# Which attention units keep whole fp32 operands, and what the plan counts for turning weights

## The chip, the cores and the metric

The kernel runs on one core of one Trainium2 chip. The metric is the device time of one execution in microseconds (us), as the median of several runs. A core has a matrix engine (PE, whose weight loads are listed apart as PEld), a vector engine (DVE), a scalar engine (ACT), GpSimd (POOL), a sync engine (SP) that issues the DMAs here, and 16 DMA engines.

## The reference, cut to what matters

```python
def _attn_ref(q, k, v, n_sink, window):          # batch 4, heads 8, sequence 768, head size 64
    scores = scale * np.matmul(q, k.transpose(0, 1, 3, 2))
    keep = is_sink | in_window                    # 4 sink columns, a causal window of 128
    scores = np.where(keep, scores, -1000000000.0)
    a = softmax(scores)
    return np.matmul(a, v)

def _moe_ref(x, w_gate, w_val, w_out):            # 3072 tokens, 512 wide, 1536 inside
    gate = 1.0 / (1.0 + np.exp(-(x @ w_gate)))
    val = x @ w_val
    return gate * val @ w_out
```

All arithmetic is to be good to fp32; the weights arrive as 64-bit floats, two 32-bit words each.

## The kernel before, in words

**Units and chunks.** Attention is cut into 96 units, numbered `u`: one head of one block of 256 queries. Eight units (the eight heads) fill one token block of 256 rows; there are 12 blocks. The feed-forward part takes the blocks in chunks (`CHUNKS`): four chunks of one block, then four of two. The chunks of two (`PAIRS`) use a scheme with sums and differences of blocks and weights, which needs further weight tiles (`thirds`) and sums of the blocks' inputs (`second_half`).

**Two ways to multiply.** An fp32 product can run on the matrix engine with whole fp32 operands, or with operands split into a high and a low part of the type fp32r, where two or three products are summed. The splitting (`copy` for the high part, `rest` for the low one) is work for ACT, DVE and POOL.

- A unit with `u < PLAIN` (line 45) is **plain**. Its queries and keys, its weights (the softmax output) and its values are whole fp32. `load` (line 875) brings 64 partitions of `qkT`; the scores of a tile are one fp32 product; `turn` (line 1043) transposes the two weight tiles and the sink columns on the matrix engine; `pv` (line 1127) multiplies, and two heads share one PSUM bank `xr`, from which the feed-forward input is taken.
- Any other unit is **split**. `load` brings 128 partitions of `qkT`, that is, twice the bytes. Then come `hi` and `kl` (lines 920 to 928), the scores as two fp32r products, `st`, `turned` and `sk` for the sinks (lines 1012 to 1035), `turn` with two transposes, a high and a low part of the weights (`wt`, lines 1071 to 1083), `vhl` (line 1093), `pv` in fp32r against the split sink values `VSHL` (line 858), and three small steps that add the parts (`low`, `xf`, lines 1155 to 1188).

**Start of the program.** While attention runs, 36 blocks of weights arrive (`wst`, three buffers) and are decoded from 64-bit floats by `decode` (line 1253): two steps on ACT (the second nearly always there), two on DVE. Chunk 0 (`feed_whole`, line 1394) multiplies with whole fp32 weights as they are decoded, and its groups of products stand ahead of those of chunk 1 in a fixed order (`GROUPS`). Its inputs `X0` sit meanwhile in one of the two buffers of `hi` and in one of `xf`. `halves` (line 1331) splits the decoded weights, and stores the low parts in DRAM (`wlo_d`), from where chunks 1 and later fetch them (`lo`).

**The order of work.** Nothing is issued in the order of the program text. A planner (`Plan`, line 313) simulates the engines with a duration that is written at each step, a priority and the buffers, and emits a fixed order for every engine. The priorities around the change: decoding 8 to 15.2, a unit its own number `u`, `halves` 16 to 25.9, the feed-forward steps of ACT, DVE and POOL below all of these numbers (first), and the matrix engine's feed-forward products last (10000 and up), so that they fill what attention leaves. The durations in the plan decide only the order; on the chip each engine runs its list and waits where it must.

**The sinks** (line 838) are stored in two tiles `VS0` for plain units, and in tiles `VSHL` for split ones, four heads each. Both kinds take the same two `vshl` buffers, so a `VSHL` tile can be filled only when the last plain unit is through.

Of the kernel before, what the change touches and what calls it, by code (L numbers as in the profile page):

```python
# [41 lines left out]
TSTEP = 8000.0  # L42
THIRDS = 130000.0
CROWDED = 350000.0
PLAIN = 20
SINKP = -2.0
SCALP = -0.5
SKSWAP = 0
# [501 lines left out]
def kernel(  # L550
# [36 lines left out]
    class Late:  # L587
# [5 lines left out]
        def tile(self, *args, **kw):  # L593
            if self.pool is None:
                first.close()
                self.pool = main.enter_context(tc.tile_pool(name="p3", bufs=1))
            return self.pool.tile(*args, **kw)
# [10 lines left out]
    plan = Plan()  # L608

    class InOrder:  # L610
# [9 lines left out]
    PE, V, A, G, Q = (  # L620
        InOrder(e) for e in (nc.tensor, nc.vector, nc.scalar, nc.gpsimd, nc.sync)
    )
# [19 lines left out]
    def dma(prio, ns, fn, r=(), w=(), start=0.0, behind=None):  # L642
        return plan.op(prio, [("Q", ISSUE, fn)], r, w, dma=ns, start=start, behind=behind)

    def copy(prio, cols, out, in_, r, w, psum=False, start=0.0, apart=False):

        plan.op(
            prio,
            [
                ("A", act(cols, psum), lambda: A.copy(out=out(), in_=in_())),  # L650
                ("V", vec(cols) if psum or apart else one(cols), lambda: V.tensor_copy(out=out(), in_=in_())),
            ],
            r, w, start=start,
        )

    def rest(prio, cols, out, in0, in1, r, w, psum=False):

        plan.op(
            prio,
            [  # L660
                (
                    "G", pool(cols), lambda: G.tensor_tensor(
                        out=out(), in0=in0(), in1=in1().bitcast(F32), op=ALU.subtract
                    ),
                ),
                (
                    "V", vec(cols) if psum else two(cols), lambda: V.tensor_tensor(
                        out=out(), in0=in0(), in1=in1().bitcast(F32), op=ALU.subtract
                    ),
                ),  # L670
            ][1 if psum else 0 :],
            r, w,
        )
# [146 lines left out]
    def zero(prio, tile, cols, ap, part=None):  # L820

        def fill():
            x = ident[128 - ap().shape[0] :, 0:1]
            while len(x.shape) < len(ap().shape):
                x = x.unsqueeze(1)
            A.mul(out=ap(), in_=x.broadcast_to(list(ap().shape)), mul=0.0)

        plan.op(
            prio, [("A", act(cols), fill)], w=[tile if part is None else (tile, part)],
        )  # L830
# [7 lines left out]
    def sinks(b, u):  # L838
        if not b:
            for y in range(2):  # L840
                for x in V0:
                    zero(u + 0.5 + y, x[y], 3 * D, lambda x=x, y=y: x[y]()[:, :, (1 - y) * D : (2 - y) * D], 4)
            for x in SK0:
                zero(u + 0.4, x, 128, x)
            for x in VS0:
                zero(u + 0.3, x, H * D, x)
            for t, x in enumerate(VS0):
                for y in range(2):
                    o = 64 * y + NS * t
                    dma(  # L850
                        u + 0.5, 91.0, lambda x=x, y=y, o=o: Q.dma_start(
                            out=x()[o : o + NS, :, y * D : y * D + D],
                            in_=v[b, y::2, 0:NS, :].rearrange("h p d -> p h d"),
                        ), w=[(x, o)],
                    )
        raw = tile([128, H, D], F32, "w2", BUFS["w2"])
        for i in range(0 if b else 1, 2):
            VSHL[b, i] = tile([128, H // 2, 2 * D], F32R, "vshl", 2, const)
        u = max(u, PLAIN) + SINKP
        for o in range(0, 128, NS):  # L860
            dma(
                u, 91.0, lambda o=o: Q.dma_start(
                    out=raw()[o : o + NS], in_=v[b, :, 0:NS, :].rearrange("h p d -> p h d"),
                ), [READY2], [(raw, o)] + [VSHL[b, i] for i in range(2) if b and (b, i) in VSHL],
            )
        for i in range(0 if b else 1, 2):
            hs = slice(i * H // 2, i * H // 2 + H // 2)
            both = VSHL[b, i]
            x, hi = lambda hs=hs: raw()[:, hs], lambda both=both: both()[:, :, 0:D]
            copy(u, H // 2 * D, hi, x, [raw], [both, READY2])  # L870
            rest(
                u, H // 2 * D, lambda both=both: both()[:, :, D : 2 * D], x, hi, [raw, both], [both]
            )
# [15 lines left out]
    def attend(u, b, h, t0, T, XR):  # L889
# [6 lines left out]
        if h == 0 and t0 == 0:  # L896
            sinks(b, u)
        plain = u < PLAIN
        y = h % 2
# [32 lines left out]
        P = tile([128, T, KW], F32, "P", BUFS["P"])  # L932
# [104 lines left out]
        tp = tile([128, 512], F32, "a", BUFS["a"], ps)  # L1037
        Z = 1 if plain else 2
        wt = tile([128, 2, T, 2, 128], F32 if plain else F32R, "wt", BUFS["w"])
# [27 lines left out]
                channel_multiplier=-1,  # L1067
            )

        plan.op(u, [("PE", 30 + (T + plain) * 110, turn)], [P], [tp, wt], busy=0.45)  # L1070
        plan.op(
            u, [("A", act(W, True), lambda: A.copy(out=w()[:, 0, :, 1], in_=tpv()))], [tp], [(wt, 0)]
        )
# [115 lines left out]
        if y:  # L1189
# [8 lines left out]
            elif not pair_of[tn]:  # L1198
# [3 lines left out]
                i = half if wide else c % 2  # L1202
# [466 lines left out]
    u = 0  # L1669
    ci = 0  # L1670
    for b in range(B):
        t0 = 0
        for T in AT[b]:
            XR = [None]
            for h in range(H):
                attend(u, b, h, t0, T, XR)
                u += 1
            t0 += T
            n = u // H - 1
            if pair_of[n]:  # L1680
                (second_half if n == CHUNKS[ci][1] else first_half)(n)
            if n == CHUNKS[ci][-1]:
                feed(ci)
                ci += 1
# [74 lines left out]
```

## Time and profile before

| | us |
|---|---|
| median of 3 runs | 773.53 |
| lowest and highest run | 773.02, 774.98 |
| span of the profiled execution | 774.4 |

The span runs from the first to the last instruction of the profiled execution. Engine times in the rows are busy times in that execution; a matrix instruction is pipelined, so its listed duration overlaps the next one's, and its real price is the distance from its start to the next start. Nearly all work shows line 618, where a helper records each operation, so the rows are told apart by tile names: `a` is a PSUM bank of attention, `m` and `o` are those of the feed-forward part, `wst` and `ws` are weights being decoded and held, `w<-o` is an output leaving PSUM.

### The profile page before, as it was taken

To read this page: it belongs to the slowest core of one execution; us is meant where nothing else is said; L and a number is where in the kernel's file an instruction comes from. 1 tells how busy PE (TensorE), PEld (TensorE's weight loads), DVE (VectorE), ACT (ScalarE), POOL (GpSimd) and SP (SyncE) were. 2 spreads that over 40 slices of the span, in tenths; PEclk is the share of its full clock that TensorE was granted. 3 is DMA by queue.
4 is the path that set the end of the run, shared out by engine and by line. 5 is a ranking of instruction groups with operands and counts; after the bars stand their busy time and mean duration, and the time that the engine had idled before them with its cause. 6 is when DMAs were issued, how large, how long until landed. Compare 5 with 4: busy or idle time off the path is not lost.

```text
span 774.4 us, 16292 instructions
## 1 busy us (share of the span) xinstructions
PE 748.7 (97%) x4986; PEld 677.2 (87%) x4986; DVE 608.8 (79%) x1781; ACT 473.2 (61%) x1338; POOL 504.3 (65%) x647
## 2 busy tenths in 40 slices
PE   7999999999899999999999999999999999999995
PEld 6877766899799899989999998999999999999994
DVE  5889988996789999968998999778999884433332
ACT  7889888665676777836656675557776652322221
POOL 3654665887899899946777987557976855311210
PEclk9999999999999999999999999999999999999999
DMA  6898987999899876776777786867697655776662
GB/s 164 225 299 255 327 255 223 358 302 307 295 316 315 281 225 217 213 255 211 239 247 232 218 257 213 255 193 245 201 302 250 192 165 180 219 238 216 192 212 79
DMA packets 120878, 185.57 MB, mean 240 GB/s; under 512 B 23248, under 2 KB 45264, under 8 KB 120784
## 3 DMA queue, kind: packets, MB, share of 16 engines
q1 hardware_dynamic: 120784, 184.45, 75.6%
q8 instruction: 42, 0.69, 0.4%
q14 instruction: 52, 0.43, 0.2%
HBM read 159.24 MB, written 25.17 MB: 238 GB/s over the span
## 4 chain that ended last, share of the span: by engine, by line
PE 59%; DVE 10%; DMA 9%; POOL 3%; ACT 2%; issue 1%; SPq 0%; POOLq 0%; ACTq 0%; DVEq 0%
PE m L618 32%; PE a L618 16%; PE o L618 10%; DMA lo<-wlo_d 3%; DMA out_dram<-w 2%; DVE ws L618 2%; DMA qkT<-in_qk_dram 2%; DVE P L618 1%; DMA vraw<-in_vt_dram 1%; POOL ws L618 1%; DVE th L618 1%; POOL wt L618 1%; DVE hi L618 1%; DMA wst<-in_moe_w_val_dram 1%; DVE xf L618 1%
## 5 line engine op out<-in xcount | busy, mean ns | idle before, releaser
L618 PE MATMUL m<-ws,ws 128*128 128x256 f32 x1536 | 290.2, 285 | 0.2 <-ACT th L618 0.2
L618 PE MATMUL m<-ws,lo 128*128 128x256 f32 x1344 | 288.8, 283 | 1.7 <-DMA lo<-wlo_d 1.6
L618 PEld LDWEIGHTS m<-ws,ws 128*128 128x128 f32 x1536 | 246.1, 190 | 11.9 <-issue 0.5
L618 PEld LDWEIGHTS m<-ws,lo 128*128 128x128 f32 x1344 | 215.6, 189 | 2.6 <-DMA lo<-wlo_d 2.5
L618 POOL TENSOR_SCALAR_AFFINE_SELECT wt<-wt 128x512 fp32r<-128x512 f32 (+3 forms) x192 | 124.9, 652 | 43.2 <-DVE wt L618 19.4
L618 POOL TENSOR_TENSOR gl<-th,gh 128x512 fp32r<-128x512 f32 (+1 forms) x34 | 38.1, 1121 | 102.2 <-ACT gh L618 83.5
L618 ACT ACTIVATE P<-P,negm_all 128x144 f32<-128x144 f32 x192 | 79.0, 412 | 30.4 <-DVE negm_all L618 29.3
L618 ACT ACTIVATE th<-m 128x256 f32<-128x256 f32 x96 | 36.7, 382 | 76.1 <-DVE th L618 71.3
L618 DVE TENSOR_TENSOR cv<-m,cv 128x256 f32<-128x256 f32 x96 | 40.1, 418 | 50.0 <-ACT cv L618 32.8
L618 ACT CAST gh<-th 128x512 fp32r<-128x512 f32 (+1 forms) x82 | 42.9, 523 | 54.2 <-DVE th L618 52.5
L618 POOL TENSOR_TENSOR ws<-ws,ws 128x512 fp32r<-128x512 f32 (+1 forms) x53 | 65.0, 1232 | 14.4 <-DVE ws L618 9.0
L618 PE MATMUL o<-ws,gh 128*128 128x512 f32 x168 | 67.7, 403 | 2.6 <-ACT w L618 2.6
L618 DVE CUSTOM_DVE_ANT_0 P<-a,am 128x144 f32<-128x144 f32 x192 | 58.3, 306 | 12.1 <-PE a L618 5.4
L618 PE MATMUL o<-ws,gl 128*128 128x512 f32 x168 | 66.0, 394 | 0.3 <-DVE gl L618 0.3
L618 PE MATMUL o<-lo,gh 128*128 128x512 f32 x168 | 65.7, 391 | 0.0
L618 PE MATMUL a<-wt,vhl 128*128 128x256 f32 (+2 forms) x282 | 61.0, 327 | 1.1 <-POOL wt L618 0.8
L618 POOL TENSOR_TENSOR kl<-qkT,hi 128x400 fp32r<-128x400 f32 (+1 forms) x56 | 58.8, 1050 | 1.8
L618 PEld LDWEIGHTS a<-wt,vhl 128*128 128x128 f32 x282 | 47.3, 189 | 10.2 <-POOL wt L618 3.0
L618 ACT CAST hi<-qkT 128x656 fp32r<-128x656 f32 (+1 forms) x70 | 49.2, 703 | 10.9 <-PE a L618 8.0
L618 POOL TENSOR_TENSOR P<-P,rs 128x288 f32<-128x288 f32 x46 | 36.5, 795 | 27.9 <-DVE rs L618 24.2
L618 POOL TENSOR_TENSOR hi<-qkT,hi 64x256 fp32r<-64x256 f32 x53 | 42.0, 793 | 14.7 <-issue 4.6
L618 DVE COPY_PREDICATED a<-tri,a 128x128 f32<-128x128 int32 x160 | 45.4, 284 | 4.8 <-PE a L618 4.5
(146 smaller groups left out, 1737.2 us busy)
## 6 DMA issues: line engine op xcount, KB each, us to landing
lo<-wlo_d SPq DMA_DIRECT2D x396, 256.0 KB, 3.6
wlo_d<-ws SPq DMA_DIRECT2D x72, 256.0 KB, 4.2
qkT<-in_qk_dram SPq DMA_DIRECT2D x52, 328.0 KB, 4.1
qkT<-in_qk_dram SPq DMA_DIRECT2D x24, 264.0 KB, 3.6
wst<-in_moe_w_gate_dram SPq DMA_DIRECT2D x12, 512.0 KB, 4.7
wst<-in_moe_w_val_dram SPq DMA_DIRECT2D x12, 512.0 KB, 5.3
wst<-in_moe_w_out_dram SPq DMA_DIRECT2D x12, 512.0 KB, 5.5
out_dram<-w SPq DMA_DIRECT2D x20, 256.0 KB, 4.0
```

The costliest lines, as they stand in the source:

```text
L618: return lambda *a, **kw: tc.keep_in_program_order(op(*a, **kw))
```

## The change

`PLAIN` goes from 20 to 16: units 16 to 19 (heads 0 to 3 of the third block of batch 0) become split, where they were plain. The two lines in `sinks` make the split sink tile for heads 0 to 3 of batch 0, which no unit needed before. The last line changes the duration that the plan counts for the transposes of a unit: from 250 to 140 ns for a split one, and from 360 to 330 ns for a plain one. What is computed is the same.

```diff
-PLAIN = 20
+PLAIN = 16
...
         raw = tile([128, H, D], F32, "w2", BUFS["w2"])
-        for i in range(0 if b else 1, 2):
+        for i in range(0 if b or PLAIN <= 16 else 1, 2):
             VSHL[b, i] = tile([128, H // 2, 2 * D], F32R, "vshl", 2, const)
         u = max(u, PLAIN) + SINKP
...
-        for i in range(0 if b else 1, 2):
+        for i in range(0 if b or PLAIN <= 16 else 1, 2):
             hs = slice(i * H // 2, i * H // 2 + H // 2)
...
-        plan.op(u, [("PE", 30 + (T + plain) * 110, turn)], [P], [tp, wt], busy=0.45)
+        plan.op(u, [("PE", 20 + T * 60 + 190 * plain, turn)], [P], [tp, wt], busy=0.45)
```

## Rows read from the trace of the kernel before

**Rows 1.** The page, busy time, share of the span and instructions of each engine.
```profile
PE 748.7 (97%) x4986; PEld 677.2 (87%) x4986; DVE 608.8 (79%) x1781; ACT 473.2 (61%) x1338; POOL 504.3 (65%) x647
```

**Rows 2.** Busy us by stretch: PE, PEld, DVE, ACT, POOL, clock, DMA share, GB/s.
```profile
73.00:131.00 58.00, 54.53 (x250) 41.03 (x249) 51.16 (x126) 50.97 (x96) 36.32 (x42) 1.00 0.85 268
131.00:329.00 198.00, 193.44 (x1353) 178.28 (x1352) 176.37 (x510) 135.20 (x422) 175.95 (x219) 0.99 0.87 283
329.00:765.00 436.00, 433.74 (x3036) 404.04 (x3035) 322.69 (x936) 224.84 (x669) 256.64 (x326) 1.00 0.70 220
```

**Rows 3.** Timeline of PE, plain units (start us, duration us, instruction, count).
```profile
84.74 1.04 PE L618 MATMUL a<-wt,vhl 128*128 128x256 f32 x6
85.62 0.49 PE L618 MATMUL a<-ident,P 128*128 128x128 f32 x3
85.95 1.03 PE L618 MATMUL m<-hi,ws 128*128 128x256 f32 x4
86.81 1.08 PE L618 MATMUL a<-qkT 128*128 128x272 f32 x4
87.73 1.03 PE L618 MATMUL m<-xf,ws 128*128 128x256 f32 x4
...
90.37 1.14 PE L618 MATMUL a<-wt,vhl 128*128 128x256 f32 x6
...
91.79 1.88 PE L618 MATMUL o<-ws,th 128*128 128x512 f32 x4
```

**Rows 4.** Timeline of PE, split units.
```profile
304.29 0.64 PE L618 MATMUL a<-wt,vhl 128*128 128x512 f32 x3
...
304.88 0.40 PE L618 MATMUL m<-ws,ws 128*128 128x256 f32 x2
...
305.59 0.30 PE L618 MATMUL a<-hi 128*128 128x272 f32 x1
...
306.10 0.40 PE L618 MATMUL m<-ws,ws 128*128 128x256 f32 x2
...
306.81 0.38 PE L618 MATMUL a<-ident,P 128*128 128x128 f32 x2
306.95 0.48 PE L618 MATMUL m<-ws,ws 128*128 128x256 f32 x2
```

**Rows 5.** Groups by form, whole span (count, busy us, mean ns, idle before).
```profile
L618 ACT CAST hi<-qkT 128x656 fp32r<-128x656 f32 x48 | 35.5, 739 | 10.9 <-PE a L618 8.0 <-POOL gl L618 1.7 <-DMA qkT<-in_qk_dram 0.8
L618 ACT COPY low<-a 64x256 f32<-64x256 f32 x76 | 28.1, 370 | 14.4 <-PE a L618 12.6
L618 DVE TENSOR_TENSOR wt<-a,wt 128x256 fp32r<-128x256 f32 x76 | 31.2, 411 | 0.4 <-ACT wt L618 0.2
L618 DVE TENSOR_TENSOR low<-a,low 64x256 f32<-64x256 f32 x76 | 31.1, 409 | 3.3 <-ACT low L618 2.9
L618 DVE TENSOR_TENSOR xf<-a,low 64x256 f32<-64x256 f32 x76 | 31.3, 412 | 1.7
L618 POOL TENSOR_TENSOR kl<-qkT,hi 128x400 fp32r<-128x400 f32 x36 | 41.5, 1153 | 1.2
L618 POOL TENSOR_TENSOR hi<-qkT,hi 64x256 fp32r<-64x256 f32 x53 | 42.0, 793 | 14.7 <-issue 4.6 <-DVE xf L618 1.7 <-DVE a L618 1.6
```

**Rows 6.** Groups of ACT: the first from 58 to 95 us, the others from 95 to 131.
```profile
L618 ACT ACTIVATE P<-P,negm_all 128x144 f32<-128x144 f32 x12 | 4.8, 406 | 0.4 <-DVE negm_all L618 0.4
...
L618 ACT ACTIVATE wst<-wst 128x512 uint16<-128x512 uint16 x11 | 15.0, 1361 | 0.2
...
L618 ACT ACTIVATE P<-P,negm_all 128x144 f32<-128x144 f32 x4 | 1.6, 400 | 0.5 <-DVE negm_all L618 0.5
```

**Rows 7.** Timelines of PE and ACT around 206 us (in brackets the idle time before).
```profile
207.25 0.50 PE L618 MATMUL o<-ws,gh 128*128 128x512 f32 x1 [2.58 <-ACT w L618]
...
206.60 0.60 ACT L618 ACTIVATE w<-o 128x512 f32<-128x512 f32 x1 [3.66 <-DMA out_dram<-w]
```

**Rows 8.** DMA issues from 58 to 131 us (count, KB each, median us to landing).
```profile
qkT<-in_qk_dram SPq DMA_DIRECT2D x4, 328.0 KB, 4.9
```

## What I expect of the change, and why

> **What bounds the kernel now.** I read the busy shares first: the matrix engine is busy 97% of the span [rows 1], so at first sight every microsecond taken off it is a microsecond of the kernel. An average over stages with different limits can mislead, so I cut the span at three places that the program text gives: 73 us, where the first scores of unit 16 leave for softmax; 131 us, where the fp32 chunk 0 ends and chunk 1 may begin; 329 us, where the first pair of blocks begins [rows 2]. From 329 us on PE is busy 433.7 of 436 us and every other engine has a quarter of its time free or more: pure matrix work, the end is PE's. From 131 to 329 us PE is busy 193.4 of 198, but DVE is at 176.4 and POOL at 176.0 too, 89% each. From 73 to 131 us, where the change puts its four units, PE has 3.5 us free of 58, ACT 7.0, DVE 6.8, POOL 21.7.
>
> The stretch from 73 to 131 us has a gate at its end: chunk 1's products stand behind chunk 0's in a fixed order, and chunk 0's last product needs the last decoded weight. PE can fill that stretch with chunk 0, as far as weights are decoded, and with attention, as far as ACT, DVE and POOL have prepared it, and with nothing else. So the time of the whole is the moment of the gate, and the matrix work that is then left, and the waits behind it.
>
> Attention in that stretch goes at the pace of ACT. Twelve softmax exponentials, that is six units, ran from 58 to 95 us, and only four, two units, from 95 to 131 us [rows 6]; unit 20, the first split one, starts just there. In the second stretch the second decoding step alone holds ACT for 15.0 us [rows 6]. Decoding has the better priority, so a unit that needs more of ACT simply comes later. PE does not set that pace.
>
> **The change part by part.** *Matrix work taken away.* Price by distance between starts. A plain unit: scores 87.73 - 86.81 = 0.92, transposes 85.95 - 85.62 = 0.33, value products 85.62 - 84.74 = 0.88 for an even head and 91.79 - 90.37 = 1.42 for an odd one, mean 1.15 [rows 3]; 2.40 us. A split unit: value products 304.88 - 304.29 = 0.59, scores 306.10 - 305.59 = 0.51, transposes 306.95 - 306.81 = 0.14 [rows 4]; 1.24 us. Four units: 4 x 1.16 = 4.6 us less for PE.
>
> *Work added to the others.* Each of the four units gets on ACT the cast of queries and keys, 0.74, and the copy of the low half, 0.37, so 1.1 us; on DVE three steps of 0.41, so 1.2 us; on POOL the two largest rests, 1.15 and 0.79 [rows 5], and several smaller steps that I do not itemise, at least 1.9 us and, if these are as long again, 3.9. Times four: ACT 4.4, DVE 4.9, POOL 8 to 16 us. The new sink tile adds one cast and one rest of 256 columns once, no longer than the longest steps above (0.8 and 1.2 us). POOL's part fits into its 21.7 free us [rows 2]. ACT's and DVE's do not fit whole: ACT would stand at 51.0 + 4.4 + 0.8 = 56.2 of 58, DVE at 51.2 + 4.9 = 56.1. If they get to 93% (53.9 us, an estimate between the 88% that they have there [rows 2] and full), about 2.3 us of each stay over the gate. What stays over is a unit or so of lower priority, units 20 to 22: I take one, with bounds of none and three.
>
> *Where the matrix time goes.* The 4.6 us are freed ahead of the gate. PE finds no more attention ready, less by a unit, and catches up with the decoded weights sooner. So they turn into idle time there, 3.5 us growing to 8 or 9. Behind the gate one unit more is left: + 1.24 us, bounds 0 and 3 x 1.24 = 3.7.
>
> *The gate itself.* A split load is 328 KB [rows 8], twice a plain one by its partitions, so 4 x 164 = 656 KB more; at the 268 GB/s of that stretch [rows 2] that is 2.4 us of transfers, at a DMA share of 0.85. If nothing hides them the weights come up to 2.4 us later; if the queue's idle share takes them, nothing. A gate that comes earlier would need faster decoding, and nothing in the change takes a step from it; so below nothing is out here. I take + 0.3, nearer to nothing, since the share of 15% that is free of 58 us is 8.7 us. On SP the eight small sink loads go from priority 18 to 14 and may now pass the loads of the last decodings (14.2 to 15.2); they wait for no buffer of the units and can go at the start, as before, so I take nothing for them.
>
> *The transposes' count.* It changes no instruction. The rows give 0.14 us for a pair and 0.33 for the plain three [rows 3, 4]; the plan counted 0.25 and 0.36 and will count 0.14 and 0.33. Its matrix time shrinks by 80 x 0.11 = 8.8 us, so it will hand PE feed-forward products a little earlier and count on attention results a little earlier too. What can that be worth? The stretch from 131 to 329 us has 198 - 193.4 = 4.6 us of idle PE in all [rows 2], 2.6 of it one wait [rows 7]; behind it 2.3 us. A better order can take at most these 6.9 us, a worse one can add as much again. I take 0, between the ends.
>
> Sum, made against the profiled execution's 774.4 us: + 1.24 + 0.3 + 0 = + 1.5. The span is 0.9 us over the median of the runs shown, which is within their spread, so I lay the same difference on the median: 773.5 + 1.5 = **775.0 us**.
>
> *A rule beside it.* In the stretch from 73 to 131 us PE is busy 94% of the time and its weight loads 41.0 of 58 us, 71% [rows 2]. The Trainium skill (Perfetto Trace Analysis, Identifying the Most-Contended Engine) says that matrix busy time is no good measure of how close the engine is to its limit, and that the weight loads' busy share is better. By the 97% the sum would be 4.6 us less; by the weight loads' 71% in this stretch it would be no less, as in my sum.
>
> **The rivals.** *The matrix engine pays back in full.* If attention is in truth held up by PE in the stretch, because feed-forward and attention share it, the freed 4.6 us let it run ahead, and the end moves by all of it: 773.5 - 4.6 = 768.9; by half, 771.2. For it: 97% [rows 1], and only 3.5 us free before the gate [rows 2]. Against it: the pace of the exponentials [rows 6].
>
> *The new order takes off waits.* The wait at 206 us, where PE stood 2.58 us until ACT could take an output out of PSUM, ACT itself having stood 3.66 us for the DMA before [rows 7], hangs on what happens to be ready then. With more attention left over at 200 us, PE may fill it. Price: 2.6 us there, with my + 1.5 it gives 773.5 - 2.6 + 1.5 = 772.4; with the other small waits of the stretch up to 770.
>
> *The vector engines turn into the bound* (slower). One mechanism: work pushed over the gate arrives in the stretch up to 329 us, where DVE and POOL are at 89% [rows 2], and the pairs cannot begin before attention up to unit 47 and the sums are done. With three units pushed over, 3.7 us of matrix work and three units of vector work come with them: of the rows' steps alone 3 x 1.2 us on DVE and 3 x 1.9 on POOL [rows 5], and two or three times that with the steps that every unit has. DVE and POOL have 21.6 and 22.0 us free there [rows 2], so this costs nothing at 329 us unless their steps wait on each other in a chain; then up to 3 us of PE idling comes on top. With the gate's 2.4 us: 773.5 + 3.7 + 2.4 = 779.6, or 782.6 with the wait; with half of the first two, 776.6. The point from which it decides is a gate later than 132 us, or an idle stretch of PE over 1 us at the first pair.
>
> *The second edit does nothing to speak of*, or the plan comes out much the same; then the first alone acts, and that is the forecast.
>
> **How the numbers follow.** A measurement of this kernel can tell about 0.3%, 2.3 us, from no change: faster is below 771.2, slower above 775.9. The forecast (772 to 775.9, with 775.0 as its value) has 0.40. The full payback has 0.17, and lies below 771.2. The new order taking off waits has 0.13, of which 0.08 end below 771.2 and 0.05 within. The vector engines as the bound have 0.30, all above 775.9. So faster 0.25, same 0.45, slower 0.30. Both signs hold much: the likeliest case's own range is 772 to 777. The range that leaves out 2 in 10 goes from 770.0, which leaves about half of the payback out, to 780.0, which takes in the gate's and the three units' bounds.
>
> **What would show it.** Right: in the profile after, the stretch before the gate has PE busy less by 4 us or more, the last fp32 product of chunk 0 stands where it stood or up to 2 us later, split scores (`a<-hi`) begin before 85 us, and the exponentials of units 16 to 22 come later than before. Wrong: unit 22 is ahead of its old 131 us, or the gate comes earlier than before; then the payback is real. If the idle time of PE from 131 to 329 us is under 3 us, the order was worth more than I gave it; if it is over 7 us, the vector engines decide.

## The result, and the profile after

The changed kernel takes 777.88 us, the median of 9 runs (775.76 to 780.73); the kernel before, run beside it, 773.19 us (9 runs, 771.40 to 776.18). The ratio is 1.0051, 95% interval [1.0032, 1.0070]: slower by 4.7 us between the medians, by 3.9 us if the ratio is taken. Forecast were 775.0 us, a range of 770 to 780, and 0.30 for slower.

The profiled execution of the changed kernel has a span of 776.2 us and took 777.88 us, the median itself. The page's busy times, and under them the same three stretches as in [rows 2], with the same columns:

```profile
PE 750.6 (97%) x5018; PEld 680.5 (88%) x5018; DVE 613.0 (79%) x1784; ACT 486.3 (63%) x1379; POOL 521.9 (67%) x661
...
73.00:131.00 58.00, 54.16 (x246) 39.95 (x245) 49.78 (x119) 51.62 (x94) 41.51 (x48) 1.00 0.79 241
131.00:329.00 198.00, 193.99 (x1380) 180.42 (x1379) 185.52 (x528) 146.07 (x449) 180.13 (x226) 1.00 0.89 291
329.00:765.00 436.00, 432.89 (x3029) 402.70 (x3028) 320.72 (x932) 227.64 (x686) 259.02 (x319) 1.00 0.70 220
```

Beside [rows 1 and 2]: PE's share is the same 97%, ACT has 13 us more work and POOL 18. Not all of that is the four units': run e2 below, which changes no unit, has 10.5 us more on ACT than the second profile of before in the three stretches together, because the planner chooses anew which engine takes a step. Nothing in the averages says where 4.7 us went. That PE is as busy as before in the first stretch is an illusion, which the groups of PE by form show (the first line from 73 to 131 us, the second for the whole span; columns as in [rows 5]):

```profile
L618 PE MATMUL m<-ident 128*128 128x128 f32 x33 | 5.1, 278 | 0.7 <-ACT th L618 0.7
...
L618 PE MATMUL m<-ident 128*128 128x128 f32 x104 | 17.3, 300 | 2.1 <-POOL ident masks.py:199 1.4 <-ACT th L618 0.7
```

`m<-ident` are products of the identity with itself, which the plan puts where it finds nothing else for PE in the first part of the program; nothing uses them. Before, there were 52 in all and none from 73 to 131 us. Without these 5.1 us PE did 49.1 us of work in that stretch, 6.0 less than the 55.1 of the second profile of before (below). About 1.4 us of the 6.0 is only later: chunk 0's last four products now stand behind 131 us.

**A second profile of before.** The first one [rows 1 to 8] had a span of 774.4 us. Another execution of the same program (run e4) has 771.6 and took 773.38 us, next to the median; the comparisons below are made with it. Its stretches:

```profile
73.00:131.00 58.00, 55.14 (x253) 41.27 (x251) 50.27 (x129) 51.16 (x97) 38.73 (x44) 1.00 0.85 272
131.00:329.00 198.00, 194.86 (x1378) 179.83 (x1377) 180.76 (x514) 134.96 (x421) 178.97 (x221) 1.00 0.87 283
329.00:765.00 436.00, 430.90 (x3011) 400.83 (x3009) 320.42 (x930) 224.75 (x668) 253.51 (x321) 1.00 0.70 220
```

**The gate.** The timeline of PE around it, first before (e4), then after (start us, duration us, instruction, count; in brackets the idle time ahead). `xf,w` and `o<-ws,th` are the last products of chunk 0, and `m<-ws,ws` is the first of chunk 1:

```profile
126.53 1.03 PE L618 MATMUL m<-xf,w 128*128 128x256 f32 x4
128.27 0.40 PE L618 MATMUL a<-hi 128*128 128x272 f32 x1 [0.71 <-POOL hi L618]
...
128.88 0.40 PE L618 MATMUL m<-ws,ws 128*128 128x256 f32 x2
...
129.62 1.88 PE L618 MATMUL o<-ws,th 128*128 128x512 f32 x4
```

```profile
129.59 1.03 PE L618 MATMUL m<-xf,w 128*128 128x256 f32 x4
130.46 1.28 PE L618 MATMUL m<-ident 128*128 128x128 f32 x10
132.19 1.98 PE L618 MATMUL o<-ws,th 128*128 128x512 f32 x4 [0.46 <-DVE ws L618]
...
134.88 0.48 PE L618 MATMUL m<-ws,ws 128*128 128x256 f32 x2
```

Before, the last weight had been decoded by 125.7 us (its row stands below); PE stood 0.71 us for POOL, which was preparing a split unit's queries and keys, and began chunk 1 ahead of chunk 0's last four products. After, it fills 1.28 us with products that nothing uses, then stands 0.46 us for DVE, which is still decoding the last weights, and chunk 1 begins 6.0 us later.

Decoding is a link in a chain. Lines of the chain that ended last, in the first profile of before (start us, duration us, what):

```profile
115.79 0.80 DVE ws L618 x2
116.59 5.48 DMA wst<-in_moe_w_val_dram
...
122.09 0.69 ACT w L618
...
122.88 1.10 ACT wst L618
...
125.22 1.12 DVE ws L618
...
126.65 0.66 DVE ws L618
...
128.15 1.69 POOL hi L618
```

The transfer of a weight block begins where a decoding step of DVE ends: there are three `wst` buffers, and a new block needs a free one. Then it passes ACT and DVE. So a step that is put in front of a decoding on ACT or DVE can hold up the next transfer too, though either engine is only 88% busy there. From this one chain that is an argument (the changed kernel's own chain does not pass this stretch); e6 below tries it.

**A ledger for all runs.** I read the starts of all PE instructions from each trace. *Gate* is the moment from which only chunk 1 and later stages are left: the first product of chunk 1, plus the price of chunk 0's products that still follow it. *Attention* is the attention work of PE behind that moment. *Waits* is the time by which the distances between starts behind it exceed the usual price of their form. The ratio is the time against the kernel before, run beside each. All other matrix work behind it is 521.0 to 521.2 us in every kernel, so the last matrix instruction starts at the sum of the three plus 521.1. In us:

| run | gate | attention | waits | last PE start | ratio of times [95%] |
|---|---|---|---|---|---|
| before, first profile | 131.8 | 83.0 | 30.0 | 765.9 | |
| before, second (e4) | 130.2 | 82.9 | 29.0 | 763.1 | (one run) |
| **after** | 134.9 | 83.9 | 27.8 | 767.8 | 1.0051 [1.0032, 1.0070] |
| e1 16, old count | 133.1 | 83.7 | 31.1 | 769.1 | 1.0072 [1.0045, 1.0098] |
| e2 20, new count | 136.7 | 81.8 | 24.0 | 763.6 | 0.9988 [0.9964, 1.0013] |
| e3 less matrix work | 131.9 | 82.8 | 28.7 | 764.4 | 0.9994 [0.9973, 1.0015] |
| e5 loads doubled | 142.4 | 82.8 | 28.0 | 774.3 | 1.0117 [1.0087, 1.0147] |
| e6 vector work added | 136.4 | 83.1 | 29.5 | 770.1 | 1.0053 [1.0033, 1.0073] |
| e7 24, old count | 142.1 | 80.9 | 42.8 | 787.0 | 1.0278 [1.0251, 1.0306] |
| e8 20, count 5 ns more | 132.7 | 82.4 | 31.8 | 768.1 | 1.0048 [1.0028, 1.0067] |
| e9 16, count 5 ns more | 134.0 | 84.5 | 31.9 | 771.5 | 1.0082 [1.0050, 1.0115] |
| e10 20, count between | 135.7 | 82.0 | 35.3 | 774.1 | 1.0159 [1.0127, 1.0192] |
| e11 16, count between | 133.3 | 83.6 | 35.6 | 773.5 | 1.0155 [1.0124, 1.0186] |
| e12 less split work | 131.9 | 83.9 | 28.6 | 765.5 | 1.0026 [0.9996, 1.0055] |

After against e4: gate + 4.7, attention + 1.0, waits - 1.2, other + 0.1 or so, in sum the + 4.7 of the last start. **Set against e4, the time is lost before 135 us, at the gate, and on balance nothing behind it.** Which edit loses it is another question: e2 has a later gate and no loss. The two profiles of the same program differ by 1.6 us at the gate and 1.0 in waits, so a row of this table is good to about that; the ratios are from many runs. (In the five rows with before's order the price of chunk 0's four trailing products comes out some 0.4 us short, since part of it shows only at the product after them. With it, after against e4 is + 4.3 at the gate and - 0.8 in waits.)

In four of the kernels part of the loss is the matrix engine's clock. The granted clock, in parts of full speed and as the mean of all their runs, is 0.990 in e5, 0.988 in e7 and 0.993 in e10 and e11, against 0.996 in the kernel before. Of 773 us that is up to 4.5, 6.0 and some 2.3 us, an estimate from these means. In the others the same estimate gives 1.2 us or less.

**When the gate began to slip.** 36 times DVE finishes the decoding of a weight block. The starts of the 3rd, 15th, 27th and 36th of these steps, in us:

| run | 3rd | 15th | 27th | 36th |
|---|---|---|---|---|
| before, first / second | 28.2 / 27.5 | 64.7 / 64.0 | 100.9 / 99.8 | 126.6 / 125.0 |
| after | 32.6 | 72.5 | 103.8 | 131.5 |
| e1 16, old count | 27.9 | 64.9 | 102.1 | 129.4 |
| e2 20, new count | 33.0 | 72.8 | 105.8 | 132.1 |
| e6 vector work added | 29.4 | 66.8 | 106.7 | 131.2 |
| e12 less split work | 31.7 | 71.6 | 102.7 | 128.2 |

The rows of DVE's timeline behind the first and last columns, one fence for each of e4, after, e2 and e1:

```profile
27.47 1.48 DVE L618 SCALAR_TENSOR_TENSOR ws<-wst,ws 128x512 int32<-128x512 int32 x1
...
125.00 0.69 DVE L618 SCALAR_TENSOR_TENSOR ws<-wst,ws 128x512 int32<-128x512 int32 x1
```

```profile
32.62 1.14 DVE L618 SCALAR_TENSOR_TENSOR ws<-wst,ws 128x512 int32<-128x512 int32 x1
...
131.47 0.67 DVE L618 SCALAR_TENSOR_TENSOR ws<-wst,ws 128x512 int32<-128x512 int32 x1
```

```profile
32.95 1.12 DVE L618 SCALAR_TENSOR_TENSOR ws<-wst,ws 128x512 int32<-128x512 int32 x1
...
132.13 0.69 DVE L618 SCALAR_TENSOR_TENSOR ws<-wst,ws 128x512 int32<-128x512 int32 x1
```

```profile
27.89 1.50 DVE L618 SCALAR_TENSOR_TENSOR ws<-wst,ws 128x512 int32<-128x512 int32 x1
...
129.40 0.73 DVE L618 SCALAR_TENSOR_TENSOR ws<-wst,ws 128x512 int32<-128x512 int32 x1
```

In the changed kernel decoding is 5.1 us late at 33 us already, before the scores of unit 16 begin (70.0 us). The new count does that, since e2 has the same lag and e1 none. (In another order the n-th step need not be the same block: e2's lag at the 3rd to 6th steps is 5.5, 3.6, 1.4 and 6.9 us.) With the old count (e1) the lag grows only in the stretch of units 16 to 19, to 4.4 us at the last decoding. So the new count alone delays the last decoding by 7.1 us against e4, the four units alone by 4.4, and both together by 6.5, each read from one profile: they don't add up.

### The profile page after: what moved, and what is told of

Its sections match the earlier page's. It is cut to its first block, busy times and chain, and to the rows that moved or that the text cites. A ratio compares the mean times of both kernels' runs of the same rounds, so it can differ in the third digit from the quotient of the medians.

```text
span 776.2 us, 16453 instructions
## 1 busy us (share of the span) xinstructions
PE 750.6 (97%) x5018; PEld 680.5 (88%) x5018; DVE 613.0 (79%) x1784; ACT 486.3 (63%) x1379; POOL 521.9 (67%) x661
## 4 chain that ended last, share of the span: by engine, by line
PE 68%; DVE 7%; DMA 2%; ACT 1%; issue 1%; SPq 0%; DVEq 0%; ACTq 0%
PE m L618 37%; PE a L618 18%; PE o L618 12%; DVE ws L618 2%; DVE th L618 1%; DMA out_dram<-w 1%; DMA lo<-wlo_d 1%; DVE sk L618 1%; DMA w<-in_v_dram 1%; DVE vhl L618 0%; DVE P L618 0%; ACT P L618 0%; DVE st L618 0%; DVE xf L618 0%; DVE gl L618 0%
## 5 line engine op out<-in xcount | busy, mean ns | idle before, releaser
L618 POOL TENSOR_SCALAR_AFFINE_SELECT wt<-wt 128x512 fp32r<-128x512 f32 (+3 forms) x192 | 127.3, 664 | 41.6 <-DVE wt L618 23.4
L618 POOL TENSOR_TENSOR gl<-th,gh 128x512 fp32r<-128x512 f32 (+1 forms) x35 | 40.9, 1167 | 87.5 <-ACT gh L618 78.1
L618 DVE TENSOR_TENSOR cv<-m,cv 128x256 f32<-128x256 f32 x96 | 40.4, 421 | 47.0 <-ACT cv L618 27.8
L618 POOL TENSOR_TENSOR ws<-ws,ws 128x512 fp32r<-128x512 f32 (+1 forms) x54 | 68.2, 1267 | 2.6 <-ACT ws L618 2.0
L618 POOL TENSOR_TENSOR kl<-qkT,hi 128x400 fp32r<-128x400 f32 (+1 forms) x60 | 66.1, 1103 | 1.9
L618 POOL TENSOR_TENSOR hi<-qkT,hi 64x256 fp32r<-64x256 f32 x56 | 45.5, 813 | 23.4 <-ACT hi L618 5.7
L618 ACT CAST hi<-qkT 128x656 fp32r<-128x656 f32 (+1 forms) x68 | 47.6, 700 | 7.3 <-PE a L618 4.9
L618 PE MATMUL a<-hi 128*128 128x272 f32 (+1 forms) x160 | 46.9, 303 | 1.6 <-DVE negm_all L618 0.7
```

What stands on the lines that cost most here:

```text
L618: return lambda *a, **kw: tc.keep_in_program_order(op(*a, **kw))
```

## The experiments

Theories at the start: the **forecast** (freed matrix time goes idle, one unit more is left behind the gate), with the **engines** (ACT and DVE delay the gate by their added work); the **order**, which any change of a counted duration reshuffles; and the **payback** of matrix time, which the result had made unlikely. In the expectations of e1 and e2, A is the first two together, B the order and C the payback.

**e1 and e2: each edit alone.** e1 has `PLAIN = 16` and the two lines for the sink tile, and the old count; e2 has only

```diff
-        plan.op(u, [("PE", 30 + (T + plain) * 110, turn)], [P], [tp, wt], busy=0.45)
+        plan.op(u, [("PE", 20 + T * 60 + 190 * plain, turn)], [P], [tp, wt], busy=0.45)
```

Expected of e1:

> PLAIN is 16, and the plan counts the transposes as before (250 and 360 ns). Theory A, work pushed over the gate: four split units put about 5 us more on ACT and on DVE before 131 us, decoding and units 20 to 22 come later, the first product of chunk 1 starts 3 to 5 us later than in the kernel before (130.7 us there), and the time is 3 to 5 us above the kernel before, so this edit alone gives the whole loss. Theory B, the plan's order: the four units cost nothing by themselves, and the loss comes from the transposes' count; then this kernel is within 1.5 us of the kernel before. Theory C, matrix payback: 3 to 4.6 us faster.

Expected of e2:

> PLAIN is 20, and only the plan's count of the transposes is changed (140 and 330 ns). Theory A: within 1.5 us of the kernel before, with the decoding of weights on its old times. Theory B: 3 to 5 us slower; the decoding of the weights is late by 4 to 5 us from the ninth block on, as it is in the changed kernel (fetch of the ninth block at 45.2 us where the kernel before has 39.4), because that lateness is there long before unit 16 begins.

Measured: e1 1.0072, 779.80 us; e2 0.9988, 773.58 us. The first edit alone gives the slowdown (the intervals of e1 and of the changed kernel overlap), and chunk 1 starts at 133.1 us, 4.2 later than in e4, as A had it. Of e2, A had the time right and the decoding wrong, B the decoding right and the time wrong. The second alone gives nothing, and this nothing is a difference of large terms: its gate is 6.5 us later than e4's, 1.1 us of attention more is done ahead of it, and 5.0 us of waits behind it are gone. With the first edit on top (after) the gate is 1.8 us earlier than e2's, but 2.1 us more of attention and 3.8 us more of waits stand behind it. So with the new count the four units cost 5.9 us behind the gate and give 1.8 back at it; with the old one, e1 against e4, they cost 2.9 us at the gate and 2.9 behind it. Where the loss stands depends on the count that it is read at.

**e3: less matrix work before the gate.** Before's order, but PE leaves out part of the value products of units 8 to 19, 7.9 us of its work.

```diff
+                if 8 <= u < 20:
+                    return
```

> The kernel before with its order on every engine unchanged, where the plain units 8 to 19 leave out part of their value products: only the first of three blocks of keys is multiplied, and no sinks, so 0.44 us of matrix time is left out in an even head and 0.88 in an odd one, 7.9 us in all, and nothing else. If matrix work ahead of chunk 1 sets the time (payback), it is 6 to 8 us faster. If the decoding of weights closes that stretch (my forecast), it is within 1 us. Between the two: the last block of chunk 0's value weights is decoded at 124.9 us in the kernel before, and with 1.73 us of up products, 0.8 us of the gate and 1.73 us of down products chunk 0 could end at about 129.2 us, where it ended at 133.4: then 4 us is the most that can be had.

Measured: 774.12 us, ratio 0.9994. The busy times of the page and the first stretch:

```profile
PE 742.5 (96%) x4914; PEld 668.1 (87%) x4914; DVE 607.0 (79%) x1781; ACT 472.6 (61%) x1338; POOL 505.1 (65%) x647
...
73.00:131.00 58.00, 53.56 (x221) 37.72 (x219) 53.34 (x131) 52.85 (x98) 36.41 (x42) 1.00 0.84 271
```

Over the whole span the waits of PE (as in the ledger, but from the start) are 57.1 us, against 47.6 in e4: 9.5 us more, for 7.9 us of work less (some 1.5 us of the 9.5 is the clock, an estimate from the 3 us that e3's profile ran at half clock; see the last section). So an engine that is busy 97% of the time gave back nothing of what was taken off it ahead of the gate. This ends the payback rival.

**e4: the kernel before again**, for a second profile; its stretches stand above.

> The kernel before once more, for a second profile. If the wait of 2.6 us at 206 us and the 3.4 us at half the clock behind it belong to the order of the work, they stand in this profile too. If they are an accident of the first profile, this span is 2 to 3 us shorter than 774.4 us, nearer to 771.5, and the stretch from 199 to 212 us shows no half clock.

Measured: a span of 771.6 us; the wait at that place is 1.07 us (its row stands in the next part), and the granted clock is 1.00 from 199 to 212 us. The long wait and the half clock were an accident of the first profile.

**e5: twice the load bytes for units 16 to 19**, in before's order, to price the bytes.

```diff
+            for _ in range(2 if 16 <= u < 20 else 1):
+                Q.dma_start(out=qkT()[0:R, 0:n], in_=qk[b, h, 0:R, c0 : c0 + n])
```

> The kernel before, its order unchanged, but units 16 to 19 fetch their 64 partitions of queries and keys twice, one after the other: the 656 KB that the split units bring more, and nothing else. Theory bytes: the transfers close the stretch before chunk 1, so its first product starts 2 to 2.5 us later than in the second profile of before (129.1 us) and the time is about 2 us higher. Theory engines (ACT and DVE with the longer chain of a split unit): within 1 us of the kernel before.

Measured: 783.97 us, ratio 1.0117, the gate 12.2 us later. But it doesn't price bytes. Two rows of the queue's timeline on SP, and one of its waits (in total, times, longest):

```profile
52.53 5.14 SPq L618 DMA_DIRECT2D qkT<-in_qk_dram  x2
...
61.66 7.40 SPq L618 DMA_DIRECT2D qkT<-in_qk_dram  x2
```

```profile
SPq L618 <- DMA qkT<-in_qk_dram: 19.3, 7, 6.3
```

The second load into the same tile waited on the queue until the first had landed (19.3 us in all, against 0.4 in e4), and the loads of weights behind it waited too. What the run shows is another thing: a gate that is 12.2 us late passes 11.2 us on to the end of PE, nearly one for one. The bytes as such stay unpriced. But the kept traces show no sign of them: from its issue between 58 and 131 us to its landing, a weight block takes 5.1 us on the mean in e4, 4.8 in e1 and 5.0 in the changed kernel. In e1 the DMA share of the first stretch is also lower than in [rows 2], 0.73 against 0.85:

```profile
73.00:131.00 58.00, 51.78 (x237) 38.52 (x236) 51.68 (x125) 52.51 (x100) 36.51 (x45) 1.00 0.73 229
```

**e6: vector work added, order kept.** Before's order; each of units 16 to 19 gets two needless steps on DVE and two on ACT (a product by 1.0, a copy in place), for each of its two tiles.

```diff
+                for _ in range(2 if 16 <= u < 20 else 0):
+                    V.tensor_scalar(
+                        out=P()[:, t], in0=P()[:, t], scalar1=1.0, scalar2=None, op0=ALU.mult
+                    )
...
+                for _ in range(2 if 16 <= u < 20 else 0):
+                    A.copy(out=P()[:, t], in_=P()[:, t])
```

> The kernel before, its order unchanged, but in units 16 to 19 the softmax tile is copied onto itself twice on ACT and multiplied by one twice on DVE, for each of the two tiles: about 1.1 us more on ACT and 1.0 to 1.2 us more on DVE for a unit, in the unit's own chain, as a split unit has it; POOL, PE and the DMAs are as before. Theory engines: decoding's last block is 2 to 4 us later than in the second profile of before (125.0 us), chunk 1 begins 2 to 4 us later than at 129.1 us, and the time is 2 to 4 us higher. Theory order (the plan that PLAIN = 16 gives is simply a poorer one): within 1 us, since the order is that of before.

Measured: 777.86 us, ratio 1.0053, + 4.1 us. The groups of these steps from 73 to 131 us, on ACT and on DVE:

```profile
L618 ACT COPY P<-P 128x144 f32<-128x144 f32 x16 | 5.1, 317 | 1.4 <-DVE P L618 1.2
...
L618 DVE TENSOR_SCALAR P<-P 128x144 f32<-128x144 f32 x16 | 4.5, 279 | 0.6
```

5.1 and 4.5 us are about what I had worked out for the split units (4.4 and 4.9). The last decoding is 6.2 us late; 2.8 of that stood at the 15th one, before the first of the added steps ran (75.7 us), so 3.4 came with them. Chunk 1 begins 6.2 us later than in e4, more than expected, but this profile is of the slowest of the 12 runs (780.32 us). The time grows by 4.1 us on the ratio, with an interval from 2.6 to 5.6. Here no step of PE is added or taken, no transfer, and each engine's list is in the old order, so the added vector work does this. It is the one price of that work in a fixed order: ahead of the gate it costs most of what it takes on either engine. It was added to ACT, to DVE and to the unit's own chain at once, so the run doesn't tell these apart.

**e7: 24 plain units**, the opposite direction, with the old count (`PLAIN = 24`, and no split sink tile for batch 0).

> PLAIN is 24, with the plan's old count of the transposes: units 20 to 23 are plain too, 4.6 us more matrix work before chunk 1, and about 5 us less on ACT and DVE. If the engines other than PE set the moment of chunk 1, as between 16 and 20: 2 to 6 us faster than the kernel before. If PE has no more to give there (it had 6 us of waits from 73 to 131 us): no gain, or 1 to 4 us slower, and 20 is the turning point.

Measured: 795.45 us, ratio 1.0278. One row of PE's timeline accounts for nearly half of it:

```profile
163.20 0.58 PE L618 MATMUL a<-sk,vshl 128*128 128x256 f32 x1 [10.42 <-DVE vshl L618]
```

PE stands 10.4 us for the split sink tile, which can be filled only when the last plain unit is through. While it stands the granted clock falls to half (0.50 from 156 to 163 us), and it stays there from 163 to 169 us, when PE works again, so the wait costs more than its length. So this run says little about units 20 to 23 as such; neither 16 nor 24 is better than 20.

**e8 to e11: counts without a meaning.** To see what a reshuffle alone is worth: the old count with 5 ns more (e8, e9) and a count between the old and the new (e10, e11), each with 20 and with 16 plain units.

```diff
-        plan.op(u, [("PE", 30 + (T + plain) * 110, turn)], [P], [tp, wt], busy=0.45)
+        plan.op(u, [("PE", 35 + (T + plain) * 110, turn)], [P], [tp, wt], busy=0.45)
...
+        plan.op(u, [("PE", 25 + T * 85 + 150 * plain, turn)], [P], [tp, wt], busy=0.45)
```

> The kernel before, with every unit's transposes counted 5 ns longer in the plan (255 and 365 ns): a change without a meaning, to see what a new order alone does to the time. If the orders that the planner gives are alike, within 1 us of the kernel before. If a new order alone moves the time by 3 us or more either way, then a single comparison of two plans says little, and the loss of the change may be that.

> PLAIN is 16, and the transposes are counted 5 ns longer than in the kernel before (255 and 365 ns): the partner of the kernel with that count and PLAIN = 20, which is 1.0048 of the kernel before. If the four split units cost 4 to 6 us by their work, whatever the order: 1.010 to 1.013 of the kernel before, 781 to 783 us. If the loss of PLAIN = 16 was a matter of one order: anything from 0.998 to 1.008.

> PLAIN is 20, and the transposes are counted 195 ns for a split and 345 ns for a plain unit, half way between the two counts of the change. If the count as such mattered, it would lie between the two (both within 0.2% of the kernel before): within 1.5 us of the kernel before. If a new order is a matter of chance, as the kernel with 5 ns more suggests, it can lie 4 us off either way.

> PLAIN is 16, with 195 and 345 ns: the partner of the kernel with that count and PLAIN = 20. Work of the split units: 4 to 6 us above its partner. Order alone: its difference from its partner is of either sign.

Measured at 20: 1.0048 and 1.0159; at 16: 1.0082 and 1.0155. Five nanoseconds in a number that the chip never sees cost 0.48%, as much as the change. The count between cost 1.6% with either number of units, of which the lower clock is up to 0.3%. Of the expectations, e9 lies between its two, e10 is far outside both, and e11 shows none of the 4 to 6 us that the split units' work was to cost. Part of the loss in e10 is visible far behind the gate, where PE has not been short of work otherwise and the clock was lower too (0.98); from 565 to 675 us in e4 and in e10:

```profile
565.00:675.00 110.00, 109.98 (x774) 102.64 (x774) 82.29 (x235) 55.79 (x167) 68.21 (x84) 1.00 0.68 211
```

```profile
565.00:675.00 110.00, 107.81 (x756) 100.78 (x755) 91.16 (x272) 62.30 (x188) 76.55 (x103) 0.98 0.67 207
```

The four pairs of 16 against 20 at the same count: + 0.72% (old), + 0.63% (new: 1.0051 / 0.9988), + 0.34% (5 ns more: 1.0082 / 1.0048) and - 0.04% (between: 1.0155 / 1.0159), mean + 0.41% or 3.2 us. In the ledger the pairs differ by + 2.9, - 1.8, + 1.3 and - 2.4 us at the gate, by + 0.8, + 2.1, + 2.1 and + 1.6 in attention, and by + 2.1, + 3.8, + 0.1 and + 0.3 in waits. Only the attention left behind the gate grows every time, by one unit or two (mean 1.65 us); the gate goes either way with the order.

**e12: less split work in the changed kernel's own order.** Units 16 to 19 leave out the low parts: per unit 0.37 us less on ACT, 0.8 on DVE, 2.4 on POOL, 0.5 on PE.

```diff
+        lite = 16 <= u < 20
...
-            pairs = (qs, kh), (qs, kl)
+            pairs = ((qs, kh),) if lite else ((qs, kh), (qs, kl))
...
+            if lite:
+                silent()
```

> The changed kernel with its order on every engine, where units 16 to 19 leave out the low parts: the rests of queries and keys and the second score product, the low part of the weights and its half of the value product, and the two steps that add the halves (the last step copies instead). For a unit that is 0.37 us less on ACT, 0.8 us less on DVE, some 2.4 us less on POOL and 0.5 us less on PE. Theory engines: chunk 1 starts 1.5 to 4 us earlier than in the changed kernel (135.3 us there) and the time is 1 to 4 us lower, 774 to 777 us. Theory order: within 1 us of the changed kernel's 777.9 us.

Measured: 776.43 us, ratio 1.0026 [0.9996, 1.0055]. The first stretch, where DVE is busy 2.6 and POOL 5.1 us less than in the changed kernel:

```profile
73.00:131.00 58.00, 53.83 (x248) 40.08 (x246) 47.19 (x112) 51.15 (x95) 36.39 (x46) 1.00 0.79 243
```

The gate is 3.0 us earlier than the changed kernel's; about 0.9 of that stood at the 3rd decoding, where the changed kernel's profile had been through a stretch at half clock and this one had not. The time is 1.45 us less (1.9 by the ratios), with an interval that overlaps the changed kernel's. The direction agrees with e6; as a size it is inconclusive.

## Why the prediction was right and wrong

**Right: freed matrix time is worth nothing there.** From 73 to 131 us PE did 6.0 us less of useful work (at least 4 were forecast; 1.4 of it is only later), and the rest became fill and waits. e3 shows the same without the change. The Trainium skill (Perfetto Trace Analysis, Identifying the Most-Contended Engine) holds the weight loads' busy share for a better measure of the matrix engine's headroom than that of its products. In this stretch the loads stand at 71%, the products at 94% [rows 2], and e3, where work taken off the engine gave nothing (0.9994), agrees. The exponentials answer to [rows 6] as forecast, later; the first line is from 58 to 95 us, the second from 95 to 131:

```profile
L618 ACT ACTIVATE P<-P,negm_all 128x144 f32<-128x144 f32 x10 | 4.0, 403 | 0.0
...
L618 ACT ACTIVATE P<-P,negm_all 128x144 f32<-128x144 f32 x6 | 2.4, 405 | 0.0
```

Unit 22, which I had named as the mark of a payback if it came ahead of 131 us, begins its exponentials at 141.2 us, against 129.8 in e4.

**Right: one unit more behind the gate.** Forecast + 1.24 us, bounds 0 and 3.7; measured + 1.0 against e4, and + 0.8 to + 2.1 in the four pairs. 76 value products with split sinks stand behind the gate, and 75 before.

**Wrong, the step that failed: the gate, + 0.3.** Measured + 4.7 against the second profile, + 3.1 against the first. I had priced the delay by bytes alone (0 to 2.4 us) and said that ACT and DVE would be too full by some 2.3 us, but then put this excess on units of lower priority, since "decoding has the better priority". That sentence holds for the plan, which can choose by its counted durations. In e6 the list of each engine was the old one, with the new steps in it, and the decoding came later, by 3.4 us after the first of them: 5.1 and 4.5 us more on ACT and DVE cost 4.1 us of time. In e1, where the plan did know of the added work and could choose, the last decoding is 4.4 us late all the same. (The load itself was placed otherwise than I had it: of the four units' casts, 0.74 us each on ACT in my sum, the plan put one on ACT and three on DVE, where they took 0.5 us.) So much is shown: added work can move the gate, and the sum's + 0.3 held the bytes alone. That the + 4.7 of this pair is that work is not shown, since e2 has an even later gate without it.

**Wrong in its place: the count, 0 between - 6.9 and + 6.9.** In sum it is nothing (e2, 0.9988), but I looked for its effect from 131 us on, at waits of PE. It acts at 27 to 33 us already, where the decoding falls back by 5 us, and takes the same back behind the gate with 5.0 us fewer waits and 1.1 us less of attention. In the changed kernel the delay stayed and only 1.2 us of the waits went. A range around the gate would have had to hold this; mine (+ 0 to + 2.4) did not.

**Luck.** The time lies inside the stated range because the upper end, 780, was drawn from the bounds of the terms and not from the sum. The sum was + 1.5 us and the measured difference 3.9 to 4.7, and 777.9 us is outside the likeliest case's own 772 to 777. Two terms that I had put at nothing or near it, the gate and the count, each moved the gate by more than the whole sum.

**The base.** I laid the first profile's 774.4 us on the median and priced a rival by its wait of 2.58 us at 207 us [rows 7]. The second profile has at this place

```profile
203.39 0.50 PE L618 MATMUL o<-ws,gh 128*128 128x512 f32 x1 [1.07 <-ACT w L618]
```

and is 2.8 us shorter. A good half of that wait was that execution's own, and the rival stood on it. Behind it the first profile ran at half clock as well (0.66 on the mean from 207 to 212 us), which is another part of its 2.8 us.

**The rivals.** Full payback: excluded (e3). New order taking off waits: real in e2 (- 5.0 us), but paid for at the gate by the same order; it gave no gain. Vector engines as the bound: its point of decision, a gate later than 132 us, was passed (134.9), and its times (776.6 to 782.6) hold the measured 777.9. But its place was ahead of the gate, in the decoding, and not in the stretch to 329 us or at the first pair: PE's idle time from 131 to 329 us is 4.0 us, against 3.1 in e4 and 4.6 in [rows 2], and from 329 us on 3.1 us, against 5.1 in e4. The 4.0 us lie between my two marks, 3 and 7. And it is not the whole story, since the new count had delayed the decoding before the added vector work began.

**The small marks.** Split scores begin at 70.0 us (before 85 was forecast). The last products of chunk 0 start at 133.6 us, 2.7 us later than e4's and 1.1 later than the first profile's (up to 2 was forecast).

**What stays open.** How much of the 4.7 us belongs to the four units and how much to the order that came out for them. The four pairs say + 3.2 us on the mean and between - 0.3 and + 5.6, and four orders are few, and one of them shows nothing. In the ledger 1.65 us of that mean is attention left behind the gate, and the gate itself comes out at none on the mean (- 0.0 of + 2.9, - 1.8, + 1.3, - 2.4); the remaining 1.6 are waits, whose cause I have not followed. The load bytes were not tried in a clean way; the landing times under e5 speak against them. No version tried beats the kernel before by more than its interval.

## What to carry to other kernels

Price a gate by every engine that its last event goes through, and not by the transfers alone: work put on ACT and DVE ahead of it costs most of its length (4.1 us for about 5 on each), while work taken off a matrix engine that is 97% busy gave nothing (7.9 us, ratio 0.9994). Where a planner fixes the order, a changed number changes everything behind it: run a few counts that mean nothing first (here they moved the time by 0.5 and 1.6%), and credit an edit only with what it does in several orders. To price a cost by itself, add it without telling the planner, so that the order stays. And before two profiles are compared, compare their granted clocks by stretch.

## What the runs showed that I had not expected

The start of the same program is not the same from run to run. The 3rd decoding starts at 27.5 and 28.2 us in the two profiles of before, and at 29.4 in e6 and 30.0 in e3, which have the same order and had not reached the work that was changed in them by then. The clock goes with it. The stretch from 20 to 23 us in e4, then in e6, with the columns of [rows 2]:

```profile
20.00:23.00 3.00, 3.00 (x23) 2.84 (x23) 2.69 (x8) 2.89 (x9) 2.49 (x3) 1.00 0.35 75
```

```profile
20.00:23.00 3.00, 3.00 (x13) 2.72 (x12) 2.77 (x8) 1.75 (x7) 2.09 (x3) 0.50 0.34 81
```

PE is busy throughout in both, but in e6 it is granted 0.50 of full speed, that is 1.2 of 2.4 GHz, and does 13 products instead of 23. From 15 to 20 us it had been busy 2.8 of 5 us in e6, and 3.2 in e4. e3 and the changed kernel have the same stretch at half clock (0.50 and 0.53), the first profile of before, e1, e2 and e12 have not. Such a lag stays in the trace up to the gate (e6's 1.9 us at the 3rd decoding are part of its 6.2 there), so that one profile of each kernel does not settle a difference of 3 us there. And a load into a tile that was still being loaded held up all that stood behind it: in e5, with four loads doubled, SP's queue stood 19.3 us for it.
